# Gated linear attention and a hard-swish MLP on one core: keys and queries transposed into scratch tiles in token pairs, growth products over alpha, and a newly searched order

## The chip, the cores and the metric

The kernel runs on one core of one Trainium2 chip. The metric is the device time of one execution in microseconds (us); the times given are medians of a few runs. The engines are named as in the profile: PE (TensorE matmuls), PEld (its weight loads), DVE (VectorE), ACT (ScalarE), POOL (GpSimd), SP (SyncE, which issues DMAs).

## The reference

Two blocks follow each other. The first is a gated linear recurrence over 768 tokens for 4 batches of 8 heads with 48 channels; the second is an MLP with a hard-swish over the 3072 tokens that come out.

```python
# q, k, v, alpha: (4, 8, 768, 48) float32
for t in range(S):
    state = alpha[:, :, t, :, None] * state + einsum('bhd,bhe->bhde', k[:, :, t], v[:, :, t])
    y[:, :, t] = einsum('bhd,bhde->bhe', q[:, :, t], state)
x = y.transpose(0, 2, 1, 3).reshape(3072, 384)
h = x @ w_in                       # w_in (384, 2048), float64 on input
g = h * clip(h + 3, 0, 6) / 6
return g @ w_out                   # w_out (2048, 384), float64 on input
```

## The kernel before

**Chunks and groups.** The 3072 tokens are 24 chunks of 128 (six per batch), and two chunks make one of 12 groups. A chunk's attention yields 128 rows of `x`; a group's 256 rows go through the MLP. Channels are laid out in four pairs of heads (`NP`), each pair on 2 x 64 partitions of which 2 x 48 are used.

**One chunk's attention, by steps.** Each step has a short name, used in the order below. `la`, `lk`, `lq`, `lv` load alpha, k, q and v (DMAs issued by SP). For chunks 0 to 5 `ta`, `tk`, `tq` transpose on PE into PSUM; from chunk 6 (`FIRST`) on a tile comes in four blocks of 32 tokens, block v holding every fourth token (`quads`, two buffers per name), and DVE transposes 32 x 32 squares from SBUF to SBUF: `by_blocks` (L286) writes block v to every fourth position, so that consecutive elements of a written row are 16 bytes apart. `ca` places alpha in `aX` (two buffers, `j % 2`), which has one leading column of zero for each pair of heads (129 columns each). `r` (`decay`, L309) runs a reverse scan that gives `R`, the product of the alphas behind each token, and puts 1/R of the first column into `ini` (L313). `p` (`growth`, L320) runs a forward scan over alpha that starts from `ini` and gives the growth products `P`. `k` and `q` (`scaled`, L332) multiply the transposed k by R and the transposed q by P; from chunk 6 on this happens in place in the tiles `Ks`, `Qs` (two buffers). Then `sc` (L346, 32 small matmul records on PE) forms scores by half chunks, `m` (L356, four DVE operations) masks them, `qa` (ACT) places q beside them, `kt` (L391, a DVE transpose with contiguous writes), `kw` and `kr` (DMAs through DRAM) bring the scaled k back by token, `u` (L430, PE) and `sm` (DVE) update the state, `st` (L409, POOL) decays it, `sv` (ACT) places it, `ya`, `yb` (L456, 64 records on PE) form y, and `cy` (ACT) keeps it.

**The MLP.** The weights come as float64 bits and are made float32 by `d1`, `d2`, `dx` (ACT), `d3` (L203 to L210, DVE) and `d4` (POOL). The first groups run plainly (`f`, `b`); from group 2 on the first product is done as 20 block products `M` (L603, eight PE records of 0.111 us each) on sums of x (`xc`, DVE) and of weights (`y`, DVE), with `n` (ACT), `o` (DVE), `e` (ACT) and `h` (DVE) behind them, and the second as seven block products `P.g.i` (L706, 16 PE records each) on sums `s` (L650, L667, DVE), with `K`, `G` and the stores `O` behind them.

**The order.** Nothing is scheduled by the compiler: one list of 1798 words (`q.8` is step `q` of chunk 8, `M.4.11` is product 11 of group 4, a last number often names a PSUM bank or a buffer) is issued as written, and each engine executes its own instructions in that order, waiting on semaphores where a producer or a reader of a buffer on another engine is not done. Attention of later chunks is woven between the MLP products of earlier groups. On PE, the small matmuls of `sc`, `u`, `ya`, `yb` stand in groups between the large ones of `M` and `P`.

Of the kernel before, what the change touches and what calls it, by code (L numbers as in the profile page):

```python
# [8 lines left out]
FP = mybir.dt.float32  # L9
# [8 lines left out]
def kernel(  # L18
# [86 lines left out]
    aX, ini = [], []  # L105
    for r in range(2):
        t = consts.tile([C, NP * W + 1], FP, tag=f"ax{r}")
        nc.vector.memset(t, 0.0)
        aX.append(t)
        t = consts.tile([C, NP * W], FP, tag=f"ini{r}")  # L110
        nc.vector.memset(t, 0.0)
        ini.append(t)
# [114 lines left out]
    Ps = consts.tile([C, NP * W], FP, tag="P", name="P")  # L227
# [46 lines left out]
    def transposed(name, j, i=None):  # L274
        if j >= FIRST:
            t = (K_t if name == "k" else Q_t)[j] = (Ks if name == "k" else Qs)[j % 2]
            by_blocks(t, name, j)
            return
        t = bank("t" + name, j, i)
        src = ring[name, j % NR]  # L280
        for p in range(NP):
            nc.tensor.transpose(
                t[:, p], src[:, 2 * p : 2 * p + 2].rearrange("s h d -> s (h d)"), ident)

    def by_blocks(to, name, j):
        nc.vector.transpose(out=to.rearrange("r p (u v) -> r p v u", v=V),  # L286
                            in_=quads[name, j % NQ][:, :, :, 0:BLK])

# [5 lines left out]
    def without_first(t):  # L294
        return t[:, 0 : NP * W].rearrange("r (p w) -> r p w", w=W)[:, :, 1:W]
# [8 lines left out]
    def decay(j):  # L304

        n = NP * W
        ax, ic = aX[j % 2], ini[j % 2]
# [5 lines left out]
        nc.vector.reciprocal(out=ic.rearrange("r (p w) -> r p w", w=W)[:, :, 0:1],  # L313
                             in_=R_t[j][:, :, 0:1])

    def growth(j):

        n = NP * W
        P_t[j] = Ps
        nc.vector.tensor_tensor_scan(  # L320
            out=P_t[j], data0=aX[j % 2][:, 0:n], data1=ini[j % 2], initial=0.0,
            op0=ALU.mult, op1=ALU.add)

    def scaled(name, j):

        if j < FIRST:
            src = ps_t.pop(("t" + name, j))
            t = (Ks if name == "k" else Qs)[j % 2]
        else:
            src = t = (K_t if name == "k" else Q_t)[j]  # L330
        by = R_t[j][:, :, 1:W] if name == "k" else without_first(P_t.pop(j))
        nc.vector.tensor_tensor(out=t, in0=src, in1=by, op=ALU.mult)  # L332
        (K_t if name == "k" else Q_t)[j] = t
# [423 lines left out]
    with tc.manual_schedule():  # L757
# [14 lines left out]
               d2.8 cy.3 d3.8 fr.0.6.1 w.9 ca.6 w.4 fr.0.7.0 fg.0.7 lv.4.1 ck.4 d2.9 d3.9 f.1.1.1  # L772
               q.4 st.4 d1.9 fr.1.1.0 fg.1.1 sv.4.0 f.1.0.2 ca.5 sc.4.1.0 u.4.1.0 fg.0.6 r.5 d1.4
               f.1.7.0 r.6 f.1.3.3 d4.8 d2.4 w.10 tk.5.3 d4.9 w.11 dx.4 fr.1.7.1 sm.4.0 d3.4 w.12
               d2.10 qa.4.0 fg.1.7 fr.1.3.1 m.4 lq.5 d1.10 f.1.6.0 d3.10 d1.12 d4.4 fr.1.0.0 f.1.2.1
               p.5 fg.1.3 d2.12 k.5 fg.1.0 d3.12 d4.10 fr.1.6.1 sm.4.1 tq.5.1 sv.4.1 lk.6 w.13
               fr.1.2.0 d1.11 f.1.4.2 d2.11 d4.12 fg.1.6 q.5 d3.11 p.6 d2.13 la.7 fr.1.4.1 fg.1.4
               f.1.5.0 lv.5.0 qa.4.1 fg.1.2 kb.5.3 fr.1.5.1 w.15 d4.11 d2.15 ca.7 ya.4.1 qa.5.1 tk.6
               yb.4 sc.5.2.0 b.1.0.2 lk.7 k.6 d3.13 d3.15 st.5 ck.5 fa.4.3 m.5 b.1.1 lq.6 w.14 tq.6
               fb.4 fg.1.5 d1.13 d1.15 d4.15 q.6 b.0.0.1 d2.14 fr.0.4.0 d3.14 y.5 d4.13 cy.4 fg.0.4  # L780
               d1.14 d4.14 x.0 y.1 y.10 b.0.1 y.0 y.2 u.5.2 P.1.0.0 K.1.0 qa.5.0 sv.5.0 qa.6.1
               P.1.1.3 b.0.2 b.1.2 kb.6.0 ya.5.3 y.6 s.1.0.0 sm.5.0 sv.5.1 G.1.0.0 tk.7 s.1.1.1
               s.1.2.3 x.1 yb.5 cy.5 b.1.3 sc.6.1.2 lv.6.2 ck.6 u.6.3.0 s.1.3.2 x.2 P.1.2 b.0.3
               K.1.1 y.7 s.1.4 s.1.5 y.11 y.3 r.7 xc.2.1 x.3 y.4 y.8 xc.2.3 k.7 xc.2.0 xc.2.4 y.9
               y.12 y.16 y.13 y.15 P.1.3.3 K.1.2 P.1.4 bo.1 P.1.5 xc.2.5 G.1.1.1 P.1.6 y.14 y.17
               la.8 xc.2.2 xc.2.6 y.19 G.1.3.3 so.1 y.20 G.1.2.2 y.18 M.2.0.2 bo.0 y.21 M.2.15.3
               y.23 sm.6.0 n.2.0.8 z.1.3 M.2.1 M.2.16 xc.2.8 n.2.1.9 xc.2.7 M.2.2 kb.7.3 p.7 lk.8
               O.1.2 lq.7 xc.2.10 sm.6.1 n.2.2.10 ca.8 m.6 M.2.7.0 lq.8 n.2.7.11 M.2.3 M.2.4 M.2.8
               xc.2.9 lv.7.0 r.8 n.2.4.12 tk.8 ck.7 lv.12.1 k.8 M.2.18.1 sv.6.1 o.2.0.0 st.7 M.2.5
               tq.7 kt.8 kw.8 n.2.5.13 M.2.9 q.7 o.2.1.0 sv.6.0 lq.9 o.2.4.0 u.7.1.3 sc.7.1.3 sm.7.0  # L790
               sv.7.0 O.1.3 M.2.10 ya.6.2 yb.6 e.2.1.1 la.9 h.2.1 e.2.0.0 y.22 lv.8.2 p.8 n.2.10.14
               qa.7.0 M.2.11 sv.7.1 M.2.6.2 n.2.18.10 M.2.19 h.2.0 n.2.11.15 qa.7.1 m.7 O.1.1 M.2.12
               cy.6 o.2.6.0 o.2.5.0 ya.7.1 yb.7 n.2.12.12 kr.8 xc.3.2 y.24 M.2.13 lv.9.0 o.2.3.0
               n.2.13.12 cy.7 tq.8 lq.10 sm.7.1 o.2.3.1 M.2.17 o.2.2.0 e.2.3.0 M.2.14 o.2.2.1 xc.3.1
               xc.3.3 la.10 e.2.2.1 P.2.0.1 xc.3.4 xc.3.5 lk.10 xc.3.6 M.3.0.2 q.8 u.8.1.0 lk.9
               sc.8.2.3 n.3.0.12 M.3.1 h.2.2 e.2.5.1 h.2.3 xc.3.0 xc.3.7 o.2.6.1 e.2.6.0 M.3.7.0
               n.3.1.9 o.2.7.0 o.2.7.1 K.2.0.3 h.2.6 M.3.2 P.2.1 qa.8.0 n.3.7.13 e.2.4.0 n.3.2.10
               xc.3.10 xc.3.8 st.8 h.2.5 ca.9 M.3.3 O.1.0 qa.8.1 h.2.4 r.9 s.2.0.14 G.2.0.1 e.2.7.0
               h.2.7 s.2.1.11 xc.3.9 M.3.4 n.3.4.8 s.2.2.15 M.3.8 P.2.3.3 o.3.0.0 K.2.2 tk.9
               s.2.3.14 s.2.5 k.9 e.3.0.1 M.3.9 o.3.1.0 M.3.5 kt.9 n.3.5.11 P.2.2 sm.8.0 s.2.4 la.11  # L800
               K.2.1 M.3.10 M.3.18.2 P.2.5 sm.8.1 e.3.1.0 n.3.18.15 tq.9 m.8 M.3.19 n.3.10.14 p.9
               M.3.11 ca.10 h.3.0 sv.8.0 q.9 kw.9 qa.6.0 G.2.2.0 kr.9 n.3.11.8 h.3.1 o.3.6.0 sv.8.1
               qa.9.0 P.2.4 o.3.5.0 sc.9.0.1 u.9.2.3 qa.9.1 M.3.12 r.10 n.3.12.10 M.3.15.2 st.9
               tk.10 m.9 M.3.16 M.3.6.3 sv.9.0 G.2.1.2 M.3.13 sm.9.0 o.3.7.0 O.2.2 ya.8.0 yb.8
               o.3.4.0 o.3.3.0 sv.9.1 k.10 ya.9.2 yb.9 n.3.13.10 cy.8 kt.10 sm.9.1 M.3.14 ca.11 cy.9
               o.3.6.1 e.3.5.0 xc.4.1 h.3.5 O.2.1 xc.4.3 xc.4.4 xc.4.0 xc.4.5 e.3.4.1 M.3.17 xc.4.6
               P.2.6 e.3.6.0 st.10 h.3.4 xc.4.2 xc.4.10 lk.11 kw.10 o.3.2.0 o.3.2.1 M.4.0.0 O.2.0
               G.2.3.3 e.3.2.1 xc.4.7 o.3.3.1 o.3.7.1 n.4.0.10 h.3.2 xc.4.8 P.3.0.1 M.4.1 K.3.0.2
               e.3.3.1 h.3.3 n.4.1.13 tq.10 e.3.7.1 P.3.1 p.10 M.4.2 q.10 kr.10 G.3.0.0 lv.10.2
               M.4.7.3 n.4.2.14 la.12 h.3.6 M.4.3 n.4.7.15 h.3.7 lk.12 s.3.0.9 M.4.4 n.4.4.8  # L810
               s.3.1.11 lv.11.0 M.4.8 r.11 P.3.3.2 sc.10.0.2 sv.10.0 s.3.2.12 o.4.0.0 u.10.1.3 tk.11
               O.2.3 M.4.9 s.3.3.9 P.3.2 p.11 K.3.2 k.11 K.3.1 s.3.5 M.4.5 qa.10.0 kt.11 o.4.1.0
               s.3.4 M.4.10 n.4.10.9 m.10 ca.12 P.3.5 sm.10.0 e.4.0.0 lq.11 n.4.5.11 xc.4.9 r.12
               kw.11 M.4.11 G.3.2.1 h.4.0 tq.11 e.4.1.1 la.13 sm.10.1 tk.12 qa.12.0 sv.10.1 M.4.18.0
               P.3.4 n.4.18.12 q.11 kr.11 sv.12.0 M.4.19 G.3.1.3 o.4.6.0 n.4.11.8 M.4.12 o.4.5.0
               st.11 k.12 qa.10.1 u.11.0 lq.12 h.4.1 qa.11.1 sv.11.0 sm.11.0 tq.12 sc.11.1.2 sv.11.1
               la.14 n.4.12.14 kt.12 P.3.6 M.4.6.2 qa.11.0 o.4.3.0 G.3.3.2 M.4.13 m.11 n.4.13.14
               ca.13 kw.12 ya.11.1 yb.11 cy.11 ya.10.2 o.4.2.0 qa.18.0 o.4.2.1 e.4.2.1 o.4.3.1 yb.10
               M.4.15.1 p.12 cy.10 M.4.16 q.12 xc.5.1 M.4.14 e.4.3.0 xc.5.0 xc.5.3 o.4.4.0 lk.13
               O.3.3 xc.5.4 h.4.3 xc.5.5 kr.12 O.3.1 P.4.0.2 M.5.0.0 o.4.6.1 xc.5.6 e.4.4.0 xc.5.7  # L820
               xc.5.2 M.4.17 h.4.4 lv.13.2 h.4.2 e.4.5.0 n.5.0.14 o.4.7.0 e.4.6.1 u.12.3.0 sc.12.3.0
               o.4.7.1 M.5.1 K.4.0.3 h.4.5 tk.13 h.4.6 s.4.0.11 n.5.1.13 e.4.7.1 r.13 M.5.7.1 lk.14
               lq.13 s.4.2.9 P.4.1 h.4.7 xc.5.8 G.4.0.3 s.4.1.12 p.13 M.5.2 tq.13 n.5.2.15 P.4.3.3
               k.13 M.5.3 M.5.4 lq.14 s.4.3.10 K.4.2 sm.12.0 kt.13 n.5.7.8 sm.12.1 O.3.2 s.4.5
# [116 lines left out]
```

## Time and profile before

| what | us |
|---|---|
| median of 3 runs | 533.34 (533.32 to 534.0) |
| the profiled execution's own time | 533.63 |
| its span (first to last instruction) | 531.8 |
| PE busy in the span | 524.3 |
| DVE busy | 475.6 |
| ACT busy | 261.4 |
| POOL busy | 50.3 |

The granted TensorE clock was 1.0 throughout. A matmul's busy time counts its whole passage through the array, and passages overlap, so PE looks busy whenever something is in it; how fast PE works is read from the distances between the starts of its matmuls. A DVE operation's duration also overlaps the next one's a little: operations of 0.68 us that stand in a row start 0.60 us apart.

### The profile page before, as it was taken

What the parts mean: (1) busy time and instruction counts of PE and PEld (TensorE: products, weight loads), DVE (VectorE), ACT (ScalarE), POOL (GpSimd) and SP (SyncE); (2) the same over time, 40 slices, a digit from 0 to 9 for tenths busy, and PEclk for the clock granted to TensorE, in tenths of its full rate; (3) what the DMA queues carried; (4) which work ended last, traced back from release to release, by engine and by line L of the source; (5) the groups of instructions that cost most, each with busy time, mean ns of one, the idle gap of its engine ahead of it and who ended that gap; (6) DMA issues with size and microseconds to landing.
All of it is one profiled execution on the core that took longest, in us unless ns stands there. A gap on an engine that the chain in (4) does not pass through costs nothing.

```text
span 531.8 us, 15076 instructions
## 1 busy us (share of the span) xinstructions
PE 524.3 (99%) x6290; PEld 494.0 (93%) x6290; DVE 475.6 (89%) x839; ACT 261.4 (49%) x513; POOL 50.3 (9%) x71
## 2 busy tenths in 40 slices
PE   8999999999999999999999999999999999999997
PEld 5798886789999999999999999999999999999997
DVE  7999999999999999999999999998999999486471
ACT  4888875212664453542673554544454454443330
POOL 5333353100000100000000000000000000000000
PEclk9999999999999999999999999999999999999999
DMA  9999867005363253453463553443531532010000
GB/s 177 246 241 251 247 153 177 2 2 133 74 150 84 64 118 77 115 123 89 95 156 85 120 136 91 96 107 69 145 78 20 129 98 48 1 33 7 9 17 30
DMA packets 124100, 54.40 MB, mean 102 GB/s; under 512 B 83328, under 2 KB 116864, under 8 KB 124032
## 3 DMA queue, kind: packets, MB, share of 16 engines
q1 hardware_dynamic: 124032, 53.44, 42.2%
q8 instruction: 49, 0.80, 0.7%
q14 instruction: 19, 0.16, 0.1%
HBM read 44.50 MB, written 8.91 MB: 100 GB/s over the span
## 4 chain that ended last, share of the span: by engine, by line
PE 85%; DVE 7%; ACT 4%; DMA 1%; issue 1%; SPq 1%; POOL 0%; DVEq 0%; ACTq 0%
PE m_ps L706 36%; PE m_ps L603 31%; PE m_ps L479 4%; PE m_ps L517 4%; PE t_ps L456 4%; PE t_ps L346 2%; PE t_ps L430 2%; DMA rings<-in_q_dram 1%; DVE A L356 1%; ACT A L366 1%; DVE g_sb L540 1%; ACT r L495 1%; ACT raw L186 1%; DVE g_sb L499 1%; SPq L251 1%
## 5 line engine op out<-in xcount | busy, mean ns | idle before, releaser
L706 PE MATMUL m_ps<-w,g_sb 128*128 128x192 f32 x704 | 121.7, 326 | 0.0
L609 ACT COPY g_sb<-m_ps 128x512 f32<-128x512 f32 x110 | 63.5, 584 | 104.2 <-PE m_ps L603 86.4
L706 PEld LDWEIGHTS m_ps<-w,g_sb 128*128 128x128 f32 x704 | 113.7, 190 | 0.6 <-DVE g_sb L667 0.3
L706 PE MATMUL m_ps<-rings,g_sb 128*128 128x192 f32 x528 | 91.7, 327 | 0.2 <-DVE g_sb L650 0.2
L706 PEld LDWEIGHTS m_ps<-rings,g_sb 128*128 128x128 f32 x528 | 85.3, 190 | 0.6 <-DVE g_sb L650 0.5
L603 PE MATMUL m_ps<-xc,w 128*128 128x128 f32 x640 | 83.5, 277 | 0.0
L603 PEld LDWEIGHTS m_ps<-xc,w 128*128 128x128 f32 x640 | 77.9, 192 | 1.1
L495 ACT ACTIVATE r<-g_sb,half 128x512 f32<-128x512 f32 x80 | 57.0, 722 | 29.8 <-DVE g_sb L499 11.9
L499 DVE SCALAR_TENSOR_TENSOR g_sb<-r,g_sb 128x512 f32<-128x512 f32 x80 | 53.5, 682 | 8.7 <-ACT r L495 8.4
L603 PE MATMUL m_ps<-xT,raw 128*128 128x128 f32 x400 | 52.8, 277 | 0.0
L603 PEld LDWEIGHTS m_ps<-xT,raw 128*128 128x128 f32 x400 | 48.8, 192 | 0.5 <-ACT g_sb L609 0.2
L409 POOL TENSOR_TENSOR st<-sm,R 128x192 f32<-128x192 f32 x20 | 12.6, 630 | 358.2 <-DVE sm L440 300.5
L650 DVE TENSOR_TENSOR g_sb<-g_sb 128x512 f32<-128x512 f32 (+1 forms) x55 | 42.1, 792 | 3.7 <-PE m_ps L706 3.5
L603 PE MATMUL m_ps<-xT,w 128*128 128x128 f32 x320 | 42.0, 277 | 0.0
L603 PEld LDWEIGHTS m_ps<-xT,w 128*128 128x128 f32 x320 | 39.0, 192 | 0.4
L366 ACT COPY A<-q 48x256 f32<-48x256 f32 x88 | 35.4, 403 | 7.3 <-DVE q L332 6.1
L356 DVE TENSOR_TENSOR A<-t_ps,mask 64x256 f32<-64x256 f32 x96 | 36.2, 416 | 1.2 <-PE t_ps L346 0.8
L479 PE MATMUL m_ps<-xT,w 128*128 128x256 f32 x144 | 33.3, 384 | 0.5 <-POOL w L217 0.3
L603 PE MATMUL m_ps<-xc,raw 128*128 128x128 f32 x240 | 32.1, 277 | 0.1
L479 PEld LDWEIGHTS m_ps<-xT,w 128*128 128x128 f32 x144 | 26.5, 190 | 5.3 <-POOL w L217 0.9
L540 DVE TENSOR_TENSOR g_sb<-g_sb 128x512 f32<-128x512 f32 x40 | 27.2, 682 | 4.6 <-ACT g_sb L609 4.6
L309 DVE TENSOR_TENSOR_SCAN R<-t,ones 128x516 f32<-128x516 f32 x24 | 29.6, 1233 | 1.6 <-ACT t L300 1.6
(105 smaller groups left out, 726.9 us busy)
## 6 DMA issues: line engine op xcount, KB each, us to landing
raw<-in_moe_w_out_dram SPq DMA_DIRECT2D x8, 768.0 KB, 5.5
raw<-in_moe_w_in_dram SPq DMA_DIRECT2D x6, 768.0 KB, 7.3
v<-in_v_dram SPq DMA_DIRECT2D x48, 96.0 KB, 3.1
out_dram<-oh SPq DMA_DIRECT2D x44, 96.0 KB, 1.8
far<-kq SPq DMA_DIRECT2D x64, 64.0 KB, 2.2
kb<-far SPq DMA_DIRECT2D x64, 64.0 KB, 2.0
aq<-in_alpha_dram SPq DMA_DIRECT2D x36, 96.0 KB, 2.5
kq<-in_k_dram SPq DMA_DIRECT2D x36, 96.0 KB, 2.5
```

The lines of the kernel that those rows point to most:

```text
L309: nc.vector.tensor_tensor_scan(out=reverse(R, n - 1, n), data0=reverse(ax, n, n), data1=reverse(ones, n, n), initial=0.0, op0=ALU.mult, op ...
L356: nc.vector.tensor_tensor(out=to[:, a], in0=sc[a][half], in1=mask[half, half].unsqueeze(1).to_broadcast([HB, NP, HB]), op=ALU.mult)
L366: nc.scalar.copy(out=to[:, a], in_=Q_t[j][64 * a : 64 * a + D, :, half])
L456: nc.tensor.matmul(y_of(j, (i + 1) // 2, p)[:, HB * b : HB * b + HB], vb[:, p, e : e + 32], A_t[j][:, b, 2 * p + a], start=(b == 0 and i = ...
L479: nc.tensor.matmul(h[:, f], w1[:, kk, o : o + C], xT_t[g][:, kk], start=(kk == 0), stop=(kk == KT - 1))
L495: nc.scalar.activation(out=to, in_=h, func=AF.Relu, bias=half, scale=1.0 / 6.0)
L499: nc.vector.scalar_tensor_tensor(out=to, in0=r, scalar=1.0, in1=h, op0=ALU.min, op1=ALU.mult)
L540: eng.tensor_tensor(out=out, in0=in0, in1=in1, op=ALU.add if s1 > 0 else ALU.subtract)
L603: nc.tensor.matmul(acc[g][i][:, f * C : (f + 1) * C], spots[w][:, f * C : (f + 1) * C], x_of(g, x), start=(first and f == 0), stop=last, s ...
L609: nc.scalar.copy(out=slots[z], in_=acc[g][i])
L650: nc.vector.tensor_tensor(out=out, in0=in0, in1=in1, op=ALU.subtract)
L706: nc.tensor.matmul(to[g], a, rhs[:, f], start=(first and f == 0), stop=(last and f == HF - 1), skip_group_check=True)
```

## The change

For chunks 6 on, k and q are transposed by `turned` into two scratch tiles (`places`, one for k and one for q) instead of into `Ks`, `Qs`. A scratch tile keeps even and odd pairs of tokens in two halves: of four neighbouring tokens, the first two lie next to each other in the first half, the last two in the second half. Consecutive elements of a transposed row are then written 8 bytes apart instead of 16. The multiplication in `scaled` reads the scratch tile back in token order, two elements from one half and two from the other, and writes `Ks`, `Qs` contiguously. Alpha is still transposed by `by_blocks`. The growth scan of chunks 6 on writes over alpha in `aX`, and POOL sets the four leading columns back to zero after q is scaled (18 times). For chunks 0 to 5 it writes to the scratch tile of q. `Ps` is dropped, and `ini` has one buffer instead of two (one clearing less at the start). The first 200 words of the order are the same; the 1598 behind are the same steps (apart from PSUM bank and buffer numbers) in another order.

```diff
-    aX, ini = [], []
+    aX = []
...
-        t = consts.tile([C, NP * W], FP, tag=f"ini{r}")
-        nc.vector.memset(t, 0.0)
-        ini.append(t)
+    ini = consts.tile([C, NP * W], FP, tag="ini")
+    nc.vector.memset(ini, 0.0)
...
-    Ps = consts.tile([C, NP * W], FP, tag="P", name="P")
+    places = {name: consts.tile([C, NP * W], FP, tag=f"{name}t", name=f"{name}t")
+              for name in "kq"}
+    turns = {name: t[:, 0 : NP * C].rearrange("r (w p n) -> r w p n", w=2, p=NP)
+             for name, t in places.items()}
...
     def transposed(name, j, i=None):
         if j >= FIRST:
-            t = (K_t if name == "k" else Q_t)[j] = (Ks if name == "k" else Qs)[j % 2]
-            by_blocks(t, name, j)
+            turned(name, name, j)
             return
...
+    def turned(to, name, j):
+        nc.vector.transpose(
+            out=turns[to].rearrange("r w p (u b) -> r p w b u", b=V // 2),
+            in_=quads[name, j % NQ].rearrange("r p (w b) d -> r p w b d", w=2)[..., 0:BLK])
+
+    def in_pairs(to):
+        return turns[to].rearrange("r w p (u b) -> r p u w b", b=V // 2)
+
+    def pairs(x):
+        return x.rearrange("r p (u w b) -> r p u w b", w=2, b=V // 2)
...
     def growth(j):
-        P_t[j] = Ps
-        nc.vector.tensor_tensor_scan(
-            out=P_t[j], data0=aX[j % 2][:, 0:n], data1=ini[j % 2], initial=0.0,
-            op0=ALU.mult, op1=ALU.add)
+        P_t[j] = places["q"] if j < FIRST else aX[j % 2]
+        to = P_t[j][:, 0:n]
+        nc.vector.tensor_tensor_scan(out=to, data0=aX[j % 2][:, 0:n], data1=ini, initial=0.0,
+                                     op0=ALU.mult, op1=ALU.add)
 
     def scaled(name, j):
+        t = (K_t if name == "k" else Q_t)[j] = (Ks if name == "k" else Qs)[j % 2]
+        by = R_t[j][:, :, 1:W] if name == "k" else without_first(P_t.pop(j))
         if j < FIRST:
-            src = ps_t.pop(("t" + name, j))
-            t = (Ks if name == "k" else Qs)[j % 2]
-        else:
-            src = t = (K_t if name == "k" else Q_t)[j]
-        by = R_t[j][:, :, 1:W] if name == "k" else without_first(P_t.pop(j))
-        nc.vector.tensor_tensor(out=t, in0=src, in1=by, op=ALU.mult)
-        (K_t if name == "k" else Q_t)[j] = t
+            nc.vector.tensor_tensor(out=t, in0=ps_t.pop(("t" + name, j)), in1=by, op=ALU.mult)
+            return
+        nc.vector.tensor_tensor(
+            out=pairs(t), in0=in_pairs(name), in1=pairs(by), op=ALU.mult)
+        if name == "q":
+            first = aX[j % 2][:, 0 : NP * W].rearrange("r (p w) -> r p w", w=W)[:, :, 0:1]
+            nc.gpsimd.memset(first, 0.0)
...
-               d2.8 cy.3 d3.8 fr.0.6.1 w.9 ca.6 w.4 fr.0.7.0 fg.0.7 lv.4.1 ck.4 d2.9 d3.9 f.1.1.1
...
+               d2.8 d3.8 d4.8 cy.3 ck.4 q.4 f.1.7.0 fr.0.7.0 w.9 w.4 d2.9 ca.6 fr.0.6.1 st.4 fg.0.6
...
```

## The prediction

> **What bounds the kernel now.** The page comes first, for the engines' shares and the chain that ended last.
>
> ```profile
> PE 524.3 (99%) x6290; PEld 494.0 (93%) x6290; DVE 475.6 (89%) x839; ACT 261.4 (49%) x513; POOL 50.3 (9%) x71
> PE 85%; DVE 7%; ACT 4%; DMA 1%; issue 1%; SPq 1%; POOL 0%; DVEq 0%; ACTq 0%
> ```
>
> PE carries the chain. DVE's 89% is a mean over two regimes, which the windows separate (PE, PEld, DVE, ACT, POOL busy in each stretch):
>
> ```profile
> 160.00:240.00 80.00, 80.00 (x1032) 78.64 (x1032) 78.47 (x142) 37.62 (x79) 2.46 (x4) 1.00 0.41 97
> 450.00:530.00 80.00, 78.95 (x754) 78.25 (x752) 43.67 (x83) 27.88 (x56) 0.51 (x1) 1.00 0.05 15
> ```
>
> Until about 450 us DVE is 96 to 98% busy beside a full PE: the two are matched. So whether a lighter DVE buys time depends on how much PE really waits for it, and busy time doesn't tell that. The timeline of PE does, by starts (first column):
>
> ```profile
> 135.71 1.06 PE L603 MATMUL m_ps<-xT,w 128*128 128x128 f32 x8
> 136.60 1.06 PE L603 MATMUL m_ps<-xc,w 128*128 128x128 f32 x8
> 137.59 0.57 PE L430 MATMUL t_ps<-v,kb 64*48 64x48 f32 x32
> 137.98 0.66 PE L346 MATMUL t_ps<-q,k 48*64 48x64 f32 x32
> 138.57 1.16 PE L603 MATMUL m_ps<-xc,w 128*128 128x128 f32 x8
> 139.66 1.10 PE L456 MATMUL t_ps<-A,v 128*32 128x64 f32 x64
> 140.69 1.16 PE L603 MATMUL m_ps<-xT,w 128*128 128x128 f32 x8
> 141.69 1.06 PE L603 MATMUL m_ps<-xc,w 128*128 128x128 f32 x8
> ```
>
> An `M` of eight records takes 0.89 (135.71 to 136.60) when another follows. Before a group of small matmuls it takes 0.99, the first one behind a group 1.00, and one between two groups 1.09: every group costs 0.10 at each end besides its own time. These steps repeat within a few nanoseconds all along, so what is left over is waiting. From 60 us on I find 1.9 us of it: 0.35 at 72.3, 0.16 at 75.2, 0.77 between 150 and 156, 0.14 at 241.5, 0.34 at 410.9, 0.10 at 424. The largest late one, in the chain:
>
> ```profile
> 409.97 0.70 DVE g_sb L499
> 410.68 0.02 issue
> 410.70 0.70 DVE g_sb L650
> 411.40 0.04 issue
> 411.44 1.57 PE m_ps L706 x8
> ```
>
> DVE's sum `s.8.3` ends and `P.8.2` goes on. That is all a lighter DVE can give back: 1.9 us of 531.8. The rest is PE's own work, 1798 unchanged steps, and the first 60 us, which lie in the 200 unchanged words.
>
> **The change, part by part.** The rows of DVE for the operations concerned (busy, mean ns of one):
>
> ```profile
> L286 DVE STREAM_TRANSPOSE q<-qq 128x512 f32<-128x512 f32 x18 | 20.1, 1118 | 0.1
> L332 DVE TENSOR_TENSOR k<-k,R 128x512 f32<-128x512 f32 x18 | 12.3, 685 | 0.1
> L391 DVE STREAM_TRANSPOSE kq<-k 128x512 f32<-128x512 f32 x16 | 11.2, 698 | 0.1
> L210 DVE SCALAR_TENSOR_TENSOR raw<-raw,w 128x768 uint32<-128x768 uint32 x11 | 10.6, 960 | 0.4
> ```
>
> *The transposes.* 36 of them (k and q of 18 chunks) write at 8 bytes instead of 16; the trace has no transpose at 8. The ends are 698 (L391, contiguous) and 1118 (L286, 16 bytes). L210 reads and writes the high words of float64 at 8 bytes, and takes 960 for 768 elements against 685 for 512 contiguous ones: 275 for 256 more, 1.07 ns each, and 685 for 512 is 1.34 with the fixed part. A step of 8 bytes thus costs DVE nothing there. I take 698: 36 x 0.42 = 15.1 us less DVE work; the far end is 0. Nothing shows a transpose under 698.
>
> *The two multiplications.* They now read two elements from one half, two from the other. Ends: 685 as now, or 685 + 420 = 1105 if such a jump costs what L286's stride does. L210 has a jump after every two elements too, inside one row, and is nearest: 685, no change.
>
> [...]
>
> *Growth over alpha, one `ini`.* The scan keeps its form (L320, median 1.23). `r` of the next chunk must now stand behind `p` of this one, on the same engine, so it is order and no wait; one clearing of 0.49 us falls away at the start, where the chain runs through the loads until 13 us: 0.
>
> *The clearing on POOL.* 18 operations of 128x4; nearest rows 0.11 (128x1) and 0.15 (32x64): about 2.3 us on an engine 9% busy. `ca` of two chunks later, on DVE, waits for it, and the whole DVE queue behind. In the new order at least 5.9 us of DVE work lies between `q` and that `ca` (chunk 11), and the POOL operations ahead (`st`, 0.63 each) wait for state sums listed earlier than `q`. That cover hides it: 0; without it 0.15 to 0.8 each.
>
> *DMAs moved.* SP takes its queue in order, so `kr` waits there for `kw` to land (rows: 2.2 and 2.0 us), with loads behind. From the last producer ahead in SP's queue to the consumer I count at least 9.3 us of DVE work in the new order (`kr.22` behind `kw.23`), 8.5 in the old (`kr.19`), which shows no PE wait. So 0.
>
> *The new order on PE.* Small matmuls stand in 31 groups behind word 200 before, in 23 after: groups with `ya`/`yb` go from 12 to 11, those of `sc` and `u` alone from 19 to 12. One group of 128 `y` records takes 1.93 where two of 64 take 2 x 1.03, and saves one pair of ends: 2.06 - 1.93 + 0.20 = 0.33. For `sc`/`u`, 32 more records in one group cost 0.48, so two groups of 64 (0.98 + 0.20 each, 2.36) become 0.98 + 0.20 + 2 x 0.48 = 2.14: 0.22 saved. Sum 1 x 0.33 + 7 x 0.22 = **1.9 us**, at most 8 x 0.33 = 2.7, at least 8 x 0.20 = 1.6. Nothing hides these, since PE is what sets the end.
>
> *The margins.* For the waits I add up, in list order, PE's own work ahead of a product, and DVE's work up to that product's last operand (each operation at its row less 0.08, since operations of 0.68 start 0.60 apart). The differences, in us, at the places where PE waited and their likes after:
>
> | place | before | after | after, transposes at 1118 |
> |---|---|---|---|
> | `sc.5` (70 us) | 72.0 - 61.2 = 10.8 | 70.3 - 60.0 = 10.4 | 10.0 |
> | `P.2.3` (155) | 153.1 - 142.4 = 10.8 | 153.1 - 142.0 = 11.2 | 7.8 |
> | `P.4.1` / `P.4.3` (241) | 230.4 - 218.1 = 12.4 | 237.6 - 223.4 = 14.2 | 6.7 |
> | `P.8.2` (411) | 408.2 - 380.5 = 27.7 | 409.2 - 373.7 = 35.4 | 20.8 |
>
> They leave out DVE's own waits, so only the comparison counts: the level before is about where PE begins to wait. After, the margin is no smaller from 150 us on and 7.7 larger at 411; the order has spent the rest of the 15.1 us on bringing attention forward, or keeps it past 450 where nobody needs it. So I let half of the 1.9 us of waits go (0.9; ends 0 and 1.9): a new order makes its own late operands.
>
> **Sum.** Span 531.8 - 1.9 - 0.9 = 529.0. The profiled execution took 533.63, 1.8 outside the span, so 530.8 against its own; it lies 0.3 above the median 533.34, which puts the median after at **530.5**. One measurement can tell 0.2%, 1.07 us, from no change.
>
> **Rivals.**
> 1. *New waits eat the gain.* Both orders are lists fixed ahead; the old one left 1.9 us of waits, another may leave 3 or 5, because DVE, ACT and SP positions all moved (at `M.5.0` the new list has 245.2 us of DVE work ahead, not 240.9, for 1.4 more PE work). Against it: the table. Time 532.3 to 535. Chance 0.20, of it 0.14 within 0.2%.
> 2. *The pairs are not cheap*, and it ends slower: a transpose with four strides at 8 bytes stays at 1118, or the reading in pairs costs up to 0.42. The price falls on `tk`, `tq`, `k`, `q` in a DVE queue that is full until 450. It decides from 0.10 us per changed operation at `P.4.3` (1.8 us more margin, 18 transposes until there) and 0.22 at `P.8.2` (7.7 over 35). At 1118 PE is 27.7 - 20.8 = 6.9 us late there: 531.8 + 6.9 - 1.9 + 1.5 = 538.3; with both dear 27.7 - 6.7 = 21 late, 552. L210 speaks against it. Chance 0.10. [...]
> 3. *All waits go, and merging pays 2.7*: 531.8 - 1.9 - 2.7 + 1.5 = 528.7. Chance 0.04 of reaching it.
>
> **Numbers.** The forecast (529 to 532.2) has 0.66. Faster 0.66 + 0.04 = 0.70, same 0.14, slower 0.06 + 0.10 = 0.16. The range goes from 528.7 to 535.0; outside are rival 2 and the tails.
>
> **What would show it.** The k and q transposes near 0.70 and the multiplications near 0.685; DVE some 15 us less busy; PE's groups of small matmuls 23 behind word 200, with 0.89 per `M` in between; PE waits after 60 us at 1 us or so. Wrong it is if a transpose stays over 0.9, if a `ca` waits for POOL, or if PE waits 3 us or more in places where the old order had none.

## The result, and the profile after

The kernel became slower: 548.09 us (median of 5 runs, 546.93 to 549.46) against 533.34 before, a ratio of 1.0277 with a 95% interval of 1.0257 to 1.0297. The forecast was 530.5, with a range up to 535.0. The profiled execution took 546.93, its span is 545.2 us.

The page after, the same two lines as before:

```profile
PE 528.0 (97%) x6290; PEld 498.0 (91%) x6290; DVE 464.3 (85%) x838; ACT 260.3 (48%) x513; POOL 51.8 (10%) x89
PE 60%; DVE 32%; issue 3%; SPq 2%; DMA 2%; ACT 1%; DVEq 0%; ACTq 0%
```

DVE has 11.3 us less to do (464.3 against 475.6), and yet its share of the chain that ended last rose from 7% to 32%. An engine can get lighter and still be waited for more.

The windows (PE, PEld, DVE, ACT, POOL busy, granted clock, DMA share, GB/s):

```profile
160.00:240.00 80.00, 76.97 (x961) 73.91 (x961) 75.39 (x141) 35.19 (x74) 2.47 (x8) 1.00 0.47 111
240.00:400.00 160.00, 153.16 (x1976) 150.39 (x1975) 137.39 (x255) 72.29 (x154) 5.71 (x15) 0.98 0.39 92
450.00:530.00 80.00, 80.00 (x805) 79.49 (x804) 48.63 (x90) 33.49 (x67) 0.51 (x1) 1.00 0.06 18
```

PE was full from 160 to 240 before; now it lacks 3.0 us there and 6.8 in the next 160. Nothing is lost behind 450.

DVE's rows for the changed operations (busy, mean ns of one, idle before):

```profile
L291 DVE STREAM_TRANSPOSE qt<-qq 128x512 f32<-128x512 f32 x18 | 12.8, 710 | 1.6 <-DMA qq<-in_q_dram 1.5
L291 DVE STREAM_TRANSPOSE kt<-kq 128x512 f32<-128x512 f32 x18 | 12.6, 702 | 0.1
L343 DVE TENSOR_TENSOR k<-kt,R 128x512 f32<-128x512 f32 x18 | 12.3, 681 | 0.1
L343 DVE TENSOR_TENSOR q<-qt,t 128x512 f32<-128x512 f32 x18 | 12.2, 680 | 0.1
```

They cost what the prediction said: 702 and 710 for a transpose, 680 for a multiplication that reads in pairs. So the loss is not in the operations.

It is in waits of PE. Worked out from the starts of PE's matmuls as in the prediction, they come to 13.7 us after 60 us (1.8 before). The largest are 3.28 at 243.7, 2.96 at 325.8 and 1.81 at 199.0; none of the others is over 0.83. The timeline around the largest (starts, duration, what, idle time before it and who ended it):

```profile
242.93 0.95 PE L444 MATMUL t_ps<-v,kb 64*48 64x48 f32 x64
244.66 0.69 DVE L681 TENSOR_TENSOR g_sb<-g_sb 128x512 f32<-128x512 f32 x1
245.27 0.70 DVE L291 STREAM_TRANSPOSE kt<-kq 128x512 f32<-128x512 f32 x1
245.90 0.65 DVE L513 SCALAR_TENSOR_TENSOR g_sb<-r,g_sb 128x512 f32<-128x512 f32 x1
246.58 0.36 DVE L452 COPY s<-t_ps 128x192 f32<-128x192 f32 x1
246.99 1.59 PE L360 MATMUL t_ps<-q,k 48*64 48x64 f32 x32 [3.11 <-DVE s L452]
```

PE has finished `u.12.2.3` and comes to `sc.13.2.3`, which writes PSUM banks 2 and 3. `sm.12` (L452) reads `u.12` from these banks and stands ahead of `sc.13` in the list, so `sc.13` has to wait for it. `sm.12` is at its turn on DVE only at 246.58, behind a growth scan, MLP operands and a k transpose. At 325.8 it is the same pattern with `u.16.2.3`, `m.17` and bank 3.

The second loss stands right behind. One-microsecond windows over this wait (the last three figures are the granted clock, DMA's share and GB/s):

```profile
245.00:246.00 1.00, 0.00 (x0) 0.00 (x0) 1.00 (x3) 0.89 (x2) 0.00 (x0) 1.00 0.49 132
246.00:247.00 1.00, 0.01 (x1) 0.01 (x1) 0.91 (x2) 0.03 (x1) 0.00 (x0) 1.00 0.73 196
247.00:248.00 1.00, 0.86 (x22) 0.73 (x26) 0.96 (x3) 0.98 (x3) 0.43 (x1) 0.72 0.57 149
248.00:249.00 1.00, 1.00 (x24) 0.88 (x17) 1.00 (x3) 0.51 (x2) 0.09 (x1) 0.50 0.01 3
249.00:250.00 1.00, 1.00 (x7) 1.00 (x7) 1.00 (x2) 0.00 (x0) 0.00 (x0) 0.50 0.00 0
250.00:251.00 1.00, 1.00 (x7) 1.00 (x7) 1.00 (x3) 0.00 (x0) 0.00 (x0) 0.58 0.00 0
251.00:252.00 1.00, 1.00 (x11) 1.00 (x11) 1.00 (x2) 0.00 (x0) 0.00 (x0) 1.00 0.00 0
```

After the wait the granted clock is 0.72, 0.50, 0.50, 0.58: 3.4 us at half, 1.7 us lost. Behind the wait at 325.8 it is 0.68, 0.50, 0.50, 0.62, as much again. The 13.7 counts a part of this half clock a second time. In e3 below, PE issues the same matmuls in the same order at full clock; its waits are 8.4 and its span is 8.0 us less. The half clock is 3.4 of these 8.0, so the waits differ by 4.6 and are 13.0 here. Span 545.2 less waits (13.0) less half clock (3.4) is 528.8; the prediction's own floor, 531.8 less 1.9 of merging less all 1.9 of waits, was 528.0.

### The profile page after: what moved, and what is told of

Read it like the earlier page. It is cut to its first block, busy times and chain, and to the rows that moved or that the text cites. A ratio compares the mean times of both kernels' runs of the same rounds, so it can differ in the third digit from the quotient of the medians.

```text
span 545.2 us, 15070 instructions
## 1 busy us (share of the span) xinstructions
PE 528.0 (97%) x6290; PEld 498.0 (91%) x6290; DVE 464.3 (85%) x838; ACT 260.3 (48%) x513; POOL 51.8 (10%) x89
## 4 chain that ended last, share of the span: by engine, by line
PE 60%; DVE 32%; issue 3%; SPq 2%; DMA 2%; ACT 1%; DVEq 0%; ACTq 0%
PE m_ps L720 25%; PE m_ps L617 22%; DVE A L370 4%; PE m_ps L531 3%; PE m_ps L493 3%; DVE g_sb L513 3%; DVE R L321 3%; PE t_ps L470 2%; DVE g_sb L554 2%; DVE g_sb L664 2%; DVE t L287 2%; DVE t L333 2%; DMA rings<-in_q_dram 1%; DVE g_sb L558 1%; DVE xc L554 1%
## 5 line engine op out<-in xcount | busy, mean ns | idle before, releaser
L617 PE MATMUL m_ps<-xT,raw 128*128 128x128 f32 x400 | 54.7, 283 | 0.1
L617 PEld LDWEIGHTS m_ps<-xT,raw 128*128 128x128 f32 x400 | 50.3, 197 | 0.8 <-DVE g_sb L556 0.3
L617 PEld LDWEIGHTS m_ps<-xc,raw 128*128 128x128 f32 x240 | 29.9, 192 | 1.6 <-DVE xc L556 1.5
```

What stands on the lines that cost most here:

```text
L617: nc.tensor.matmul(acc[g][i][:, f * C : (f + 1) * C], spots[w][:, f * C : (f + 1) * C], x_of(g, x), start=(first and f == 0), stop=last, s ...
```

## The experiments

PE's waits are those after 60 us in the one profiled execution of each kernel, from starts. For the changed kernel and e11 the count (13.7 and 20.4) takes in some of the time at half clock, and the table gives what remains without it, from the spans against e3. Each ratio is to the kernel before on the same chip.

| kernel | median us | ratio, 95% interval | span | PE waits |
|---|---|---|---|---|
| before | 533.34 | | 531.8 | 1.8 |
| after | 548.09 | 1.0277 [1.0257, 1.0297] | 545.2 | 13.0 |
| e1: new operations, old order | 532.61 | 0.9984 [0.9974, 0.9993] | 530.8 | 1.4 |
| e2: new order, wide stride | 560.26 | 1.0496 [1.0474, 1.0518] | 558.4 | 24.0 |
| e3: two words moved | 539.90 | 1.0120 [1.0096, 1.0145] | 537.2 | 8.4 |
| e4: three words moved | 539.56 | 1.0103 [1.0083, 1.0122] | 536.0 | 6.9 |
| e5: eleven words more | 537.72 | 1.0087 [1.0066, 1.0107] | 535.0 | 6.5 |
| e6: e1, one group later | 532.68 | 0.9986 [0.9978, 0.9995] | 531.3 | 1.1 |
| e7: e5, one idle stretch filled | 536.68 | 1.0060 [1.0048, 1.0073] | 536.0 | 7.9 |
| e8: e7, three moves more | 536.86 | 1.0070 [1.0048, 1.0092] | 533.5 | 5.0 |
| e9: e8, six words more | 539.37 | 1.0115 [1.0085, 1.0146] | 534.9 | 5.9 |
| e10: e1, two merges | 533.43 | 0.9996 [0.9987, 1.0005] | 531.9 | 3.1 |
| e11: e5, attention later | 555.52 | 1.0416 [1.0395, 1.0437] | 552.4 | 17 to 18 |
| e12: e5, eight transposes left out | 535.14 | 1.0039 [1.0025, 1.0052] | 532.4 | 4.3 |

The mended orders vary by 2 to 6 us from one execution to the next (e9: 536.3 to 542.5), the old one by 1.3 to 2.4, so a span of one profile is read beside the median.

### e1: the new operations in the old order

```diff
 the changed kernel, with the list of the kernel before, but for three words
 (alpha is overwritten and ini is shared, so p goes ahead of the next r, k ahead of the next tk):
-r.6 ... p.5            -r.18 ... p.17          -tk.22 n.9.4.14 k.21
+p.5 r.6                +p.17 r.18              +k.21 tk.22
```

> All operations of the changed kernel (pairs, scratch tiles, growth over alpha, clearing on POOL, one ini) in the order of the kernel before; three words are moved because the single tiles need it (p.5 ahead of r.6, p.17 ahead of r.18, k.21 ahead of tk.22). Theory A (the operations are as cheap as priced; the loss comes from the new list, whose matmuls stand where their operands are late): DVE some 15 us less busy than before, PE waits after 60 us of at most 1.9 us, time 531.5 to 533.5. Theory B (the new operations themselves make DVE or PE wait: single scratch tiles, the clearing on POOL, the growth over alpha): over 540 in this order too.

Measured 532.61, a little faster than before. The page:

```profile
PE 523.5 (99%) x6290; PEld 494.0 (93%) x6290; DVE 464.8 (88%) x838; ACT 261.5 (49%) x513; POOL 50.9 (10%) x89
PE 86%; DVE 9%; DMA 2%; SPq 1%; issue 1%; ACT 0%; DVEq 0%; ACTq 0%
```

DVE is as light as in the changed kernel (464.8), and PE waits 1.4 us. So the 15 us come with the new order; the operations are sound, and by themselves worth 0.16%. That is all because the old order had little waiting to give back.

### e2: the new order with the old stride

```diff
-    turned(...): writes 8 bytes apart, the multiplication reads in pairs
+    writes 16 bytes apart into the scratch tile, the multiplication reads it contiguously
```

> The changed kernel with its list, scratch tiles and clearing, but k and q are turned in token order, 16 bytes apart, and read contiguously by the multiplication. Theory A: 36 transposes back at 1.12 us put 15 us back on DVE, so PE's waits grow by some 5 to 15 us over those of the changed kernel: 553 to 563. Theory B: the pairs are not what helps or hurts, 546 to 550.

Measured 560.26. The rows:

```profile
L287 DVE STREAM_TRANSPOSE kt<-kq 128x512 f32<-128x512 f32 x18 | 20.0, 1110 | 0.1
L287 DVE STREAM_TRANSPOSE qt<-qq 128x512 f32<-128x512 f32 x18 | 20.3, 1130 | 0.7 <-DMA qq<-in_q_dram 0.7
```

14 us more DVE work (busy time 478.2 against 464.3) cost 13.2 us of span (558.4 against 545.2), of which 1.7 is more half clock (10.2 us of it against 6.8). In the new order DVE's work is worth nearly its full length; in the old order e1 saved 11 us of it for 1.0 us of span.

### e3 and e4: three words

```diff
-sm.12.0 sm.12.1 sv.12.1 O.4.0 sc.13.2.3        -m.17 n.7.1.10 u.16.2.3
+sc.13.2.3 sm.12.0 sm.12.1 sv.12.1 O.4.0        +u.16.2.3 m.17 n.7.1.10
 and in e4 also
-lk.12 lq.12 e.3.6.0 kr.10 ... O.2.2 lq.11
+lq.11 lk.12 lq.12 e.3.6.0 kr.10 ... O.2.2
```

> The changed kernel with two words moved in the list: sc.13 ahead of sm.12, u.16 ahead of m.17. Each engine's own sequence of instructions stays the same; what falls away is that these matmuls wait for a DVE read of another part of the same PSUM bank. Theory A: the waits of 3.25 us at 243.7 and of 2.96 at 325.8 vanish, and with them the half clock behind each (0.50 for 3.3 us, some 1.7 us each): 9.6 less, 538.5. Rival C (DVE is the bound in those stretches, and what PE does not wait for there it waits for at the next operand): 545 to 548, with the waits a few us later.

> As the two words moved, and lq.11 ahead of lk.12, so that this load no longer stands in SP's queue behind a kr that waits for its kw to land. Theory A: the 1.8 us wait of P.3 at 199 us (DVE sat idle 1.54 for the load) vanishes too: 536.7. Rival C: as with the two words alone.

The two words of e3 took 8.2 us off the time (548.09 to 539.90; theory A had 9.6) and 8.0 off the span: 3.4 with the granted clock, which is 1.00 throughout instead of 0.993, and 4.6 in waits. Rival C's time, 545 to 548, did not come. In e3's timeline the scores follow the state sums at once (3.11 us idle ahead of them in the changed kernel), and the sum that reads the other half of the banks comes whenever DVE has time:

```profile
242.75 0.95 PE L444 MATMUL t_ps<-v,kb 64*48 64x48 f32 x64
243.51 0.68 PE L360 MATMUL t_ps<-q,k 48*64 48x64 f32 x32
246.40 0.36 DVE L452 COPY s<-t_ps 128x192 f32<-128x192 f32 x1
```

No operation changed, nor the order on DVE or on PE: the dependence is made by the place in the list, since a write of one part of a bank is held behind a read of another part that was listed earlier. The third word, `lq.11`, stood behind `kr.10` and a store in SP's queue, and q of chunk 11 came late: DVE's 1.5 us for `qq` in the row of L291 above. Moved, PE's wait at 199 fell from 1.32 (e3) to 0.16 and the span by 1.2; the median hardly moved (539.90 to 539.56), within the spread.

### e5, e7, e8, e9: mending DVE's queue by hand

```diff
 e5  xc.4.5 ahead of h.3.4; o.4.1.0 ahead of tk.13; p.13 behind o.4.7.1; tk.14 tq.14 behind s.4.2.9;
     r.15 tk.15 behind o.5.1.0; tk.21 k.21 behind G.7.2.1; r.23 p.23 behind m.21
 e7  + tq.13 ca.14 ahead of G.3.2.1
 e8  + G.4.2.0 (K.4.1, P.4.5) ahead of k.15; s.1.2.3 ahead of x.2; o.7.4.0 ahead of tq.19
 e9  + p.13 behind h.4.2; q.14 tq.15 behind o.5.5.0; kt.11 kw.11 behind s.3.1.11; r.13 behind o.4.3.0
```

> The changed kernel's operations and its order with the three words of the run before this one moved, and nine more moves on DVE's queue alone, each to put attention steps behind an MLP operand that PE waited for: xc.4.5 ahead of h.3.4; o.4.1.0 ahead of tk.13; p.13 behind o.4.7.1; tk.14 and tq.14 behind s.4.2.9; r.15 and tk.15 behind o.5.1.0; tk.21 and k.21 behind G.7.2.1; r.23 and p.23 behind m.21. DVE does exactly the same operations; only PE's waits can change. Theory A (what the new order still loses is the local order of DVE's queue, where attention stands ahead of an operand that PE needs sooner): of PE's waits of 6.9 us after 60 us the ones at 189, 211, 231 to 236, 247, 257, 382 and 424 go, about 4 us in all; span 532 to 533, time 534.5 to 536. Theory B (DVE is the bound by now and its amount of work, not its local order, sets PE's lateness): each wait comes back a few us later, time 538.5 to 540.

> The run before this one (nine local moves) with two more words moved: tq.13 and ca.14 ahead of G.3.2.1. Between 190 and 262 us DVE there had one idle stretch, 1.74 us before G.3.2.1, which waits for PE's product P.3.2; all the rest of that stretch it was full, and PE waited 1.40 at 234.8 (h.4.2) and 1.61 at 258.5 (G.4.2.0) for it. tq.13 (0.70) and ca.14 (1.12) need neither PE nor that result. Theory A (a DVE that waits for PE in a full stretch pays the idle time back later as PE's wait): the idle before G.3.2.1 falls to 0.3 or less, the waits at 234.8 and 258.5 fall by some 1.4 each (by 2.8 in all if both hang on the same lateness, by 1.5 if the first carries over to the second), span 532.2 to 533.5, time 534.5 to 536.3. Theory B (DVE's amount of work until 262 sets these waits, and the idle time is their echo): no change, 537 to 538.

> The run with tq.13 and ca.14 moved, and three more local moves: G.4.2.0 (with K.4.1 and P.4.5) ahead of k.15, s.1.2.3 ahead of x.2, o.7.4.0 ahead of tq.19, each an operand that PE waited for (1.6, 0.5 and 0.23 us). Theory A: PE's waits after 60 us come to some 2.4 us, near the 1.8 of the old order; with 23 groups of small matmuls instead of 31 the span is then 530 to 531.5, time 532 to 533.3, at or below both kernels. Theory B (the new order is DVE-bound there): 536 or more.

> The run with all moves so far, and six more, five steps on DVE's queue and the DMA behind one of them: p.13 behind h.4.2 (it stood just ahead of it, where PE waited 1.07 at 234.4), q.14 and tq.15 behind o.5.5.0 (0.96 at 260.4), kt.11 and kw.11 behind s.3.1.11 (0.42 at 199.3), r.13 behind o.4.3.0 (DVE idle 0.69 for POOL's st). The operations and their number stay the same. Theory A (each wait left is an operand that stands behind attention steps for want of a local order): those three waits go, 2.4 us, span 531 to 531.8 where the run before had 533.5, time 533 to 534.5. Theory B (DVE is the bound until 262, moves only shift the waits): waits of about the same sum appear within 10 us behind, time 536 to 537.5.

In e5 eleven words moved. It gave 537.72, between its two theories. The waits behind 300 us went as theory A said (0.86 at 382, 0.45 at 424). Those between 190 and 262 did not: the many small ones became 1.40 at 234.8 and 1.61 at 258.5. The first is in part my own doing, since `p.13` now stood just ahead of the `h.4.2` that PE needs. In that stretch DVE idled only once, for PE:

```profile
214.40 0.25 DVE L554 TENSOR_TENSOR xc<-xT,xc 128x128 f32<-128x128 f32 x1
216.38 0.36 DVE L740 TENSOR_TENSOR oh<-m_ps,u 128x192 f32<-128x192 f32 x1 [1.74 <-PE m_ps L720]
```

e7 filled this idle time to 0.44, but opened 0.69 at `r.13`, which waits for POOL's `st`. PE's wait for `h.4.2` fell from 1.40 to 1.07, the other stayed at 1.62, and 0.3 to 1.1 more appeared at 108, 199 and 271, which the moves do not explain. The median fell by 1.0. Inconclusive: the direction of theory A, a quarter of its size.

e8 took the wait for `G.4.2.0` away and met `o.5.5.0`, next in the queue, 0.96 late in its place; the median stayed (536.86), inside theory B's 536 or more. e9 did what was asked at each of its places (`h.4.2` 0.24, 199 down to 0.12, 260 gone) and got worse: `xc` late by 0.94 at 239.5, 0.70 at 269.3 behind the delayed q, 1.88 of DVE idle where the early `ca.14` waits for its load, and two of six executions with a granted clock of 0.997 (539.4 and 542.5), which those of e5 and e7 never had and those of e8 once (539.8). Theory B holds there: between 190 and 302 us there is always another operand close behind the one that is helped.

### e12: 4.8 us of DVE work left out

```diff
-            turned(name, name, j)
+            if not 12 <= j <= 15:
+                turned(name, name, j)
```

> The run with nine local moves (e5), its list unchanged, but the transposes of k and q of chunks 12 to 15 left out (tk, tq: eight DVE operations of 0.60 us each, 4.8 us; what the multiplications read there is the chunk before). It measures whether DVE's sum of work until 262 us sets PE's waits of 1.40 at 234.8 and 1.61 at 258.5, while DVE is full from 190 to 302. Theory B (the list brings more DVE work ahead of these places than DVE can do by then, and every move only shifts who is late): 2.4 us less work ahead of the first place and 4.8 ahead of the second are more than the lateness, both waits fall to 0.2 or less, DVE shows idle time between 235 and 302 instead, span 531.5 to 532.3, time 533.5 to 534.5. Theory A (the waits belong to single operands behind DMAs, ACT or POOL): they stay at 1 us or more, span 534 or more.

Without these transposes the multiplications of chunks 12 to 15 read old contents of the scratch tiles, so this kernel serves only to measure. Measured 535.14, 2.6 less than e5, span 532.4. The wait for `G.4.2.0` at 258.5 went altogether, and DVE got idle time of 0.97 at 260. The wait for `h.4.2` only fell from 1.40 to 1.07, because DVE arrives at `G.3.2.1` earlier and waits longer there:

```profile
216.11 0.36 DVE L741 TENSOR_TENSOR oh<-m_ps,u 128x192 f32<-128x192 f32 x1 [2.71 <-PE m_ps L721]
```

2.71 instead of 1.74: what DVE had gained, it lost again at a step that waits for PE, and behind it the queue is the same. So theory B holds at 258, where the amount of work decides. At 235 it does not: the wait stays over 1 us as in theory A, but it hangs on none of the DMAs, ACT or POOL that theory A named. It hangs on the order of DVE's queue behind a PE result, as e9 and e11 show, where `p.13` stands behind `h.4.2` and the wait is 0.24 and 0.27.

### e11: whole blocks of attention later

```diff
 e5  + p.13 behind h.4.2; r.14 tk.14 p.14 k.14 behind o.5.0.0; tq.14 ca.15 behind o.5.1.0;
     q.14 tq.15 r.15 tk.15 k.15 kt.15 kw.15 behind m.13; tk.16 r.16 p.16 k.16 kt.16 behind sm.15.0
```

> The run with nine local moves (e5), and the attention steps of chunks 14 to 16 on DVE put later in the list, where their consumers still have time: in e5, k of chunks 14, 15 and 16 was done 26, 20 and 39 us ahead of the scores that read it, while DVE was full from 190 to 302 us but for one idle stretch, and PE waited 1.40 at 234.8 and 1.61 at 258.5. Moved: p.13 behind h.4.2; r.14, tk.14, p.14, k.14 behind o.5.0.0; tq.14, ca.15 behind o.5.1.0; q.14, tq.15, r.15, tk.15, k.15, kt.15 and the DMA kw.15 behind m.13; tk.16, r.16, p.16, k.16, kt.16 behind sm.15.0. Operations and their number stay. Theory A (PE's waits at 230 to 260 come from attention that stands too early in the list: its sum of work is no bound, its place is): both waits fall to 0.3 or less, no new ones over 0.5, span 532 to 533, time 534 to 535.5. Theory B (moves on DVE only shift the waits, as they did in the two runs before): a new wait of 1 us or more appears at a moved step or its DMA (u.15 waiting for kr.15 near 278), time 537 or more.

Theory A's version failed: 555.52. The two waits did fall (0.27 at 234, none at 258), but the block moved behind `m.13` takes 4.8 us of DVE (263.3 to 268.1), and the MLP sums behind it were just as urgent. The timeline:

```profile
273.88 2.64 PE L720 MATMUL m_ps<-w,g_sb 128*128 128x192 f32 x8 [4.19 <-DVE g_sb L554]
```

The windows behind it:

```profile
274.00:275.00 1.00, 1.00 (x4) 1.00 (x5) 0.66 (x2) 1.00 (x3) 0.00 (x0) 0.61 0.86 172
275.00:276.00 1.00, 1.00 (x5) 1.00 (x5) 0.83 (x4) 0.42 (x2) 0.00 (x0) 0.50 0.88 218
```

Half clock followed (0.61, 0.50), and then 2.3, 0.8, 0.6 and 2.4 us at 283 to 290, for the rows of k of chunk 15, whose `kt` and `kw` came later, and of chunk 14, whose `kr` stands behind that of 15 in SP's queue. Theory B had named this wait of `u.15` for `kr.15`. Half clock followed here too, 6.8 us of it, and a third time behind a wait of 3.9 at 311 for an MLP operand: 13.7 us at half, which is 6.8 lost. Attention 20 us ahead of its use is thus no free slack: a block can go later only in pieces, between operands.

### e6 and e10: can e1 be improved

```diff
 e6   -sc.9.0.1 u.9.2.3 qa.9.1 M.3.12            e10  -M.2.10 ya.6.2 yb.6     -ya.5.3 ... yb.5 cy.5 b.1.3
      +qa.9.1 M.3.12 sc.9.0.1 u.9.2.3                 +ya.6.2 yb.6 M.2.10     +b.1.3 ya.5.3 ... yb.5 cy.5
```

> The run with the changed kernel's operations in the old order, and one group (sc.9.0.1, u.9.2.3) moved behind M.3.12, so that the rows of k of chunk 9 (kr.9) have some 0.9 us more to land; there PE waited 0.70 us at 151.7. Theory A (this wait was on that DMA alone, and the old order with cheap transposes has slack elsewhere): the wait goes, nothing else comes, span 530.1, time 531.9. Theory B (what is gained there is lost at the next operand, since DVE is as late as the DMA): time 532.6 as without the move.

> The changed kernel's operations in the old order (as in the first run), with two groups of small matmuls merged into their neighbours by moving the one product between them: M.2.10 behind yb.6, b.1.3 ahead of ya.5.3; 29 groups instead of 31 behind word 200. Theory A (each group costs 0.10 at each end, and the old order has no waits there): 2 x 0.2 = 0.4 us less, span 530.4, time 532.2. Theory B (what is saved is lost at the next operand): 532.6 as without the merges.

e6 removed the wait of 0.70 at 151.7 and found 0.17 and 0.23 at 154 to 155; its median, 532.68, is that of e1, as theory B said. e10 merged two pairs of groups for an expected 0.4 and came out at 533.43, some 0.8 above e1: `u.6` now stood before its v and k were there (0.65 at 108.8), and the product moved behind `yb.6` handed its PSUM bank over 0.84 late, at 140.5:

```profile
141.47 1.16 PE L617 MATMUL m_ps<-xT,w 128*128 128x128 f32 x8 [0.68 <-ACT g_sb L623]
```

Neither theory of e10 had that: merging isn't free, it moves operands. e1 stays the best version measured, ahead of the kernel before by little: 0.9984 [0.9974, 0.9993].

## Why the prediction was wrong, point by point

**Right: the operations.** Transposes 702 and 710 (predicted 698), multiplications 680 (685), growth over alpha no dearer in any way that PE met, POOL's clearings 0.13 each and no `ca` waiting for them. Rival 2 is refuted, and e2 prices it: 13.2 us if the transposes had stayed at 1118.

**Nearly right: the floor.** 528.8 by measurement, 528.0 worked out. Of the merging's 1.9 us, group costs taken from starts show 2.0 (45.0 us in the 31 groups of before, 43.0 in the 23 of e4). Spans less waits show less, about 1.2: 529.4 to 530.0 for e1 and before, 528.1 to 529.1 for e3, e4, e5, e8 and e12. Which of the two is right stays open.

**Too large: the DVE work saved.** 15.1 us were predicted; the rows of the k and q transposes went from 20.1 each to 12.6 and 12.8, 14.8 less. These are durations, and DVE's busy time, in which overlapping operations count once, fell by 11.3 (10.8 in e1). The reason is in the starts. A transpose of before, with the next operation right behind it:

```profile
411.91 1.08 DVE L286 STREAM_TRANSPOSE q<-qq 128x512 f32<-128x512 f32 x1
412.85 1.10 DVE L286 STREAM_TRANSPOSE t<-aq 128x512 f32<-128x512 f32 x1
```

They are 0.94 apart, and 0.95 to 0.96 in the median of all such places, 0.16 less than the duration; the prediction took 0.08 off for every operation. Behind a transpose of 0.70 the next one starts 0.63 later (245.27 to 245.90 above). So each saves 0.33 and not 0.42, 11.9 us in 36. With this, the table's gain at `P.4.1`/`P.4.3`, 1.8 us for 18 transposes, would be some 0.2.

**Wrong: the margins.** The step that failed is "So I let half of the 1.9 us of waits go". The waits rose to 13.0 instead of falling to 1.0, which is 12.0 us, and 3.4 of half clock came on top: 15.4 of the 16.2 by which the span missed 529.0. The other 0.8 is the floor. Three things were missing in that step.

*The table compared totals, and the waits were local.* It found 14.2 us at `P.4.1`/`P.4.3`, more than before, a few us from where PE then waited 3.28. The wait hung on `sm.12` behind five other operations of DVE's queue and on a bank shared in the list, neither of which enters a sum of work. The one number that spoke of this place, 245.2 us of DVE work ahead of `M.5.0` against 240.9, was put under rival 1 and overruled by the table.

*"They leave out DVE's own waits, so only the comparison counts"* assumed the same waits in both orders. DVE's idle time in front of `G.3.2.1` is 2.04 us in the changed kernel (1.74 in e5, 2.71 in e12), while the longest of before between 160 and 310 us is 0.61, and time that DVE gains ahead of such a step is not passed on.

*A late load was dismissed.* The term for DMAs that moved was put at 0 from distances of the k rows only; `lq.11`'s place behind `kr.10` cost the third largest wait.

**Rival 1 had the mechanism, and its size was off.** "Another may leave 3 or 5" had no bound behind it: it was an old order's 1.9 with a little added. The test on record fits, though: PE waits 3 us and more in places where the old order had none. e3 alone shows what a bound would have needed: two words of 1798 carry 8.2 us.

**No price for a stopped PE.** The sum had no term for the half clock, and the trace of before, with a clock of 1.0 throughout, has no such row. In the changed kernel it followed stops of 3.11 and 2.80 us and cost 1.7 each, 3.4 of the span. More on this stands in the last section.

**What stays open.** e4 leaves 6.9 us of waits, and moves by hand brought the median to 536.7 at best. That DVE is full from 190 to 302 us and that its amount of work decides at 258 is shown by e12; how an order with 23 groups would have to look to wait as little as the old one is not shown, nor whether there is one.

## What to carry to other kernels

When two engines are both nearly full, an order is a result of its own: change operations and order apart, and measure the operations in the old order first (e1). To forecast a new order, walk each large matmul group to the operation it waits for, and look at what stands ahead of that one in its own queue, at whose read of the same PSUM bank is listed before it, and at the loads in SP's queue; sums of work per engine don't see any of the three. Price an operation of a full engine by the distance to the next start, not by its duration. Look first for waits near 3 us, since two of these cost 8 us here and moving one word each removed them.

## What the hardware showed that was not expected

- A stop of PE can cost clock besides its own time. By the idle times of the timeline, single stops of 1.65 us (changed kernel, to 200.9) and 2.57 (e2, to 113.0) left the granted clock at 1.00; 2.80 (changed kernel, to 328.8), 3.11 (to 247.0), 3.12 (e2, to 339.2), 3.74 (e11, to 314.9) and 4.19 (e11, to 273.9) were each followed by some 3.4 us at 0.50. The length of one stop alone doesn't settle it: e11 stopped four times between 283.0 and 289.6, for 2.15, 0.62, 0.46 and 2.25, and the clock fell within the last of these and stayed at 0.50 for 6.8 us. A stop of 3.44 in e2 (to 255.3) brought 6.8 us as well. So these runs give no single threshold. Within e11's last stop:

```profile
288.00:289.00 1.00, 0.00 (x0) 0.00 (x0) 0.00 (x0) 0.00 (x0) 0.00 (x0) 0.50 0.74 137
```

- A transpose of 128 x 512 that writes 8 bytes apart (702 to 710) costs what a contiguous one does (L405, 700); at 16 bytes it costs 1110 to 1130, with the same input.
- Reading two elements from one half of a tile and two from the other costs a multiplication nothing: 680 against 685 contiguous.
